# Another order of words in the front and in all passes, with one first-layer tile begun on three of four pairs of heads

## The chip, the cores and the metric

The kernel runs on one core of one Trainium2 chip. The metric is device microseconds for one execution, the median of several runs. TensorE (PE) multiplies matrices and writes into PSUM, eight banks of 512 fp32 columns. VectorE (DVE) and ScalarE (ACT) read PSUM and write SBUF; GpSimd (POOL) works on SBUF alone and issues most of the loads; SyncE (SP) issues stores and transposing DMAs. Every engine runs its own instructions in the order of the program and waits for the others by semaphores.

## The reference

Four batches of eight heads, 768 rows of 64 numbers. Rows are cut into chunks of 32; a chunk attends to its own 32 keys, 16 to the left, 8 to the right and 8 memory keys of its head. The result, laid out as 3072 tokens of 512 numbers, goes through two layers:

```python
for c in range(nc):                       # chunks of 32 rows
    k_full = concat(mem_k, k[l_start:r_end]); v_full = concat(mem_v, v[l_start:r_end])
    scores = q_c @ k_full.T / sqrt(64)
    a = softmax(scores); out[c] = a @ v_full
x = out.transpose(0, 2, 1, 3).reshape(3072, 512)
h = x @ w_in                              # 512 -> 2048
g = h + sin(alpha * h) ** 2 / (alpha + 1e-9)
y = g @ w_out                             # 2048 -> 512
```

## The kernel before, in words

**Passes.** There is a front, which prepares the attention of batch 0, and four passes, one for each batch. Pass i runs the two layers of batch i, and beside them the attention of batch i+1. The first layer is 16 tiles of 128 hidden features by 768 tokens. A tile takes a pair of PSUM banks (half 0 and half 1, 384 tokens each), and each half is four matmuls over the four k-tiles of `xT`; a k-tile is a pair of heads (`half_tile`, L422). Then ACT takes the sine (`sine`, L435), one of ACT, DVE or POOL squares it (`squared`, L441), and DVE adds it to the hidden value and writes `gT` (`finish`, L449), which gives the pair of banks back. The second layer (`second`, L458) multiplies `gT` by `w_out`, 96 matmuls of 512 columns for a batch, six token tiles of sixteen, each in one bank, copied out by ACT or DVE in turn (`close`, L467) and stored by SP.

**Words.** The order of the work is written out by hand. A stage runs a string of words; each word's first letter names a method of `Stage` (L503), the rest is its argument, and each method only issues instructions on the engines that it needs. The ones that matter here:

- `a`: cast one loaded pair of heads of batch 0 to bf16 (0 to 3 keys, 4 to 7 queries; the last letter is the engine, V for DVE, A for ACT). `k`, `l`: transpose a pair of heads of keys or queries on PE. `K`, `L`: copy that out of PSUM (`put_k`, `put_q`; after every `K`, DVE copies the two ends of the row, L291).
- `C`: constants. `Cb`, `Cm` the mask bias, `Ck` the memory keys, `Cl` alpha and its inverse, `Ci`, `Cp`, `Cz`, `Cv`, `Cs` fills on POOL. `We`, `Ws`: load ACT's table for the exponential or the sine by a dummy activation (L699). `z`: matmuls on zeros, 512 columns each (L686), which compute nothing.
- `s`, `v`: scores with exponential, and values with the division (`normed`, L350). In the front the two digits are the pair of heads and the half of the tokens. `t`, `T`: transpose one block of the result into `xT` by PE and copy it by DVE or ACT; `c`: the same by a transposing DMA.
- `b`, `h`: half 0 and half 1 of a first-layer tile (`h` also issues the sine). `q`: the square, its last letter the engine. `g`: `finish`. `p`, `P`: the first three k-tiles of a half ahead of the rest (`early`, L533); the strings of before do not use them.
- `f`: that many second-layer matmuls. `o`: hand the second layer of this pass to the feed, in groups of tokens; an `f` that asks for a matmul whose `gT` is not issued yet takes none. After the last pass the rest of the feed runs.
- `V`, `U`, `I`, `d`, `R`, `Z`, `X`, `m`, `H`: loads of values, of `w_out`, of `w_in`, of queries and keys, and the memory values; `V`, `U`, `I`, `d`, `R` are DMAs issued by POOL, and so stand in one queue with POOL's squares.

**PSUM.** `Banks` (L59) hands out, at the time the program is written, the pair that was given back longest ago. With four pairs in all, the fifth open tile must wait on the chip for a `finish` of an earlier one.

Of the kernel before, what the change touches and what calls it, by code (L numbers as in the profile page):

```python
# [11 lines left out]
NEG = -30000.0  # L12
CROSSED = {0: (0, 0), 1: (0, 0), 2: (1, 1), 3: (1, 1)}
KW = 1024
BF = mybir.dt.bfloat16
F32 = mybir.dt.float32
ACTF = mybir.ActivationFunctionType
ALU = mybir.AluOpType


class Feed:
# [64 lines left out]
def kernel(  # L86
# [20 lines left out]
    KT = d_model // P  # L107
# [14 lines left out]

    ident = consts.tile([P, P], BF, name="ident")
    biasm = consts.tile([P, 6], F32, name="biasm")
    mcol = consts.tile([P, P], BF, name="mcol")
    mrow = consts.tile([P, P], BF, name="mrow")
    asum = consts.tile([P, 8], BF, name="asum")
    mind = consts.tile([P, NJ, 3, 32], BF, name="mind")
    tiny = consts.tile([1, 1], F32, name="tiny")
    zeros = consts.tile([P, 512], BF, name="zeros")  # L130
    kTs = [consts.tile([P, HP, KW], BF, name=f"kT{i}") for i in range(2)]
    qTs = [consts.tile([P, HP, S], BF, name=f"qT{i}") for i in range(2)]
# [217 lines left out]
    def normed(otv, bs):  # L350
# [5 lines left out]
            in1=rinv[:].unsqueeze(3).to_broadcast([QW, 2, HP, D]),  # L356
            op=ALU.mult,
        )
# [61 lines left out]


    def half_tile(t, hf, k0=0, k1=4):  # L422
        for kt in range(k0, k1):
            nc.tensor.matmul(  # L424
                t["hT"][:, hf, 0:HALF],
                w_in_sb[:, kt, P * t["ft"]:P * t["ft"] + P],
                t["xT"][:, kt, HALF * hf:HALF * hf + HALF],
                start=(kt == 0), stop=(kt == KT - 1),
            )

    def opened(ft, xT):
        hT, bs = banks.pair()
        return {"ft": ft, "xT": xT, "hT": hT, "bs": bs, "from": [0, 0]}
# [7 lines left out]
    def squared(t, eng):  # L441
# [3 lines left out]
        else:  # L445
            e = nc.vector if eng == "V" else nc.gpsimd
            e.tensor_tensor(out=s2[:], in0=u[:], in1=u[:], op=ALU.mult)  # L447

    def finish(t, gT):  # L449
# [3 lines left out]
            in0=t["s2"][:], scalar=inv_alpha[:, ft:ft + 1], in1=t["hT"][:, :, 0:HALF],  # L453
            op0=ALU.mult, op1=ALU.add,
        )
# [47 lines left out]
    class Stage:  # L503
# [29 lines left out]
        def early(self, a, hf):  # L533
            if int(a) not in self.tile:
                self.tile[int(a)] = opened(int(a), self.next_x() if self.i < 0 else self.xT)
            t = self.tile[int(a)]
            half_tile(t, hf, 0, 3)
            t["from"][hf] = 3
# [6 lines left out]

        def do_b(self, a):
            if int(a) not in self.tile:
                self.tile[int(a)] = opened(int(a), self.xT)
            t = self.tile[int(a)]
            half_tile(t, 0, t["from"][0])  # L550

        def do_h(self, a):
            t = self.tile[int(a)]
            half_tile(t, 1, t["from"][1])
            sine(t)
# [175 lines left out]
    def const_b():  # L731
        for col, lo, hi in rows:
            nc.vector.tensor_reduce(
                out=biasm[:, col:col + 1], in_=ident[:, lo:hi], op=ALU.add, axis=mybir.AxisListType.X
            )
        for col in (0, 3):
            nc.vector.tensor_tensor(
                out=biasm[:, col:col + 1], in0=biasm[:, col:col + 1], in1=biasm[:, 5:6], op=ALU.add
            )
        nc.vector.tensor_scalar(  # L740
            out=biasm[:, 0:5], in0=biasm[:, 0:5], scalar1=-NEG, scalar2=NEG,
            op0=ALU.mult, op1=ALU.add
        )
# [59 lines left out]
    def const_s():  # L803
# [6 lines left out]
    first = {}  # L810
    stage = Stage(-1, None)
    stage.tile = first
    stage.run((
# [3 lines left out]
    ))  # L817
    for i, words in enumerate(((
# [6 lines left out]
    ),(  # L825
# [5 lines left out]
    ),(  # L831
# [5 lines left out]
    ),(  # L837
# [3 lines left out]
    ))):  # L841
        stage = Stage(i, stage.nx).run(words)
    feed.take(400)

# [28 lines left out]
```

## Time and profile before

| | |
|---|---|
| median of three runs | 215.29 us (214.83 to 215.68) |
| span of the profiled execution | 213.1 us; the runs lie 1.8 to 2.6 us above it, the median 2.2 |
| PE busy | 201.7 us, 95% |
| ACT, DVE, POOL busy | 143.5, 140.5, 99.8 us |
| first-layer matmuls (L424) | 512 |
| second-layer matmuls (L462) | 400 |
| first matmul of a first-layer tile | 24.81 us |
| last second-layer stretch of pass 3 begins | 189.32 us |

The span runs from the first to the last instruction; no time of the profiled execution itself beyond its span is given. Matmuls overlap, so a matmul's own duration is about twice the time until the next one starts, and PE's busy share says little; what counts is when each group starts and how many matmuls it holds. The idle time shown in brackets behind a row is that of its engine just before the row, with what ended it.

### The profile page before, as it was taken

To read this page: it belongs to the slowest core of one execution; us is meant where nothing else is said; L and a number is where in the kernel's file an instruction comes from. 1 tells how busy PE (TensorE), PEld (TensorE's weight loads), DVE (VectorE), ACT (ScalarE), POOL (GpSimd) and SP (SyncE) were. 2 spreads that over 40 slices of the span, in tenths; PEclk is the share of its full clock that TensorE was granted. 3 is DMA by queue.
4 is the path that set the end of the run, shared out by engine and by line. 5 is a ranking of instruction groups with operands and counts; after the bars stand their busy time and mean duration, and the time that the engine had idled before them with its cause. 6 is when DMAs were issued, how large, how long until landed. Compare 5 with 4: busy or idle time off the path is not lost.

```text
span 213.1 us, 4479 instructions
## 1 busy us (share of the span) xinstructions
PE 201.7 (95%) x1721; PEld 113.5 (53%) x1721; DVE 140.5 (66%) x218; ACT 143.5 (67%) x230; POOL 99.8 (47%) x140
## 2 busy tenths in 40 slices
PE   0799899999999999999999999999999999999994
PEld 0456555565455556555455555554555555554443
DVE  7598678999542749975856649898157197865011
ACT  2597898976857469977846199887846289891110
POOL 8959515688598193009991039659400023200000
PEclk9999999999999999999999999999999999999999
DMA  6999999999999999969999229989945400000312
GB/s 195 337 163 141 193 209 205 204 163 182 131 177 141 137 148 144 180 88 110 126 217 171 72 63 131 156 126 129 175 115 123 124 15 0 2 3 0 148 49 98
DMA packets 95908, 28.19 MB, mean 132 GB/s; under 512 B 84864, under 2 KB 92432, under 8 KB 95888
## 3 DMA queue, kind: packets, MB, share of 16 engines
q0 software_dynamic: 68736, 13.25, 92.3%
q1 hardware_dynamic: 26976, 14.62, 28.2%
q8 instruction: 13, 0.21, 0.4%
q14 instruction: 7, 0.06, 0.1%
q10 hardware_dynamic: 176, 0.04, 0.1%
HBM read 29.66 MB, written 6.29 MB: 169 GB/s over the span
## 4 chain that ended last, share of the span: by engine, by line
PE 71%; DVE 9%; DMA 7%; ACT 4%; issue 4%; POOL 3%; DVEq 0%; POOLq 0%; ACTq 0%
PE ps L462 38%; PE ps L424 27%; DMA memv_st<-in_mem_v_dram 4%; DVE gT L451 4%; DVE s L447 3%; DMA vw<-in_v_dram 3%; PE ps L414 3%; PE ps L385 2%; ACT u L439 2%; PE ps L366 1%; ACT s L444 1%; POOL s L447 1%; POOL vw L172 1%; DVE kT L285 1%; ACT L699 1%
## 5 line engine op out<-in xcount | busy, mean ns | idle before, releaser
L462 PE MATMUL ps<-w_out_sb,gT 128*128 128x512 bf16 (+2 forms) x400 | 89.1, 371 | 0.0
L424 PE MATMUL ps<-xT,w_in_sb 128*128 128x384 bf16 x512 | 86.0, 326 | 0.7 <-DVE gT L451 0.4
L451 DVE SCALAR_TENSOR_TENSOR gT<-s,inv_alpha,ps 128x768 bf16<-128x768 f32 x64 | 63.0, 1011 | 12.5 <-ACT s L444 5.2
L424 PEld LDWEIGHTS <-w_in_sb 128*128 128x128 bf16 x512 | 49.8, 98 | 35.4 <-issue 2.1
L439 ACT ACTIVATE u<-ps,alpha_sb 128x768 f32<-128x768 f32 x64 | 56.6, 895 | 16.8 <-PE ps L424 14.3
L462 PEld LDWEIGHTS <-gT 128*128 128x128 bf16 x400 | 36.6, 98 | 37.9 <-DVE gT L451 0.2
L447 POOL TENSOR_TENSOR s<-u 128x768 f32<-128x768 f32 x11 | 17.4, 1582 | 69.7 <-ACT u L439 69.7
L399 ACT ACTIVATE pt<-ps,biasm 128x256 bf16<-128x256 f32 x72 | 27.2, 489 | 10.5 <-PE ps L385 10.5
L469 DVE COPY o_sb<-ps 128x512 f32<-128x512 f32 (+1 forms) x15 | 10.1, 678 | 28.3 <-PE ps L462 26.4
L447 DVE TENSOR_TENSOR s<-u 128x768 f32<-128x768 f32 x23 | 21.9, 953 | 7.8 <-ACT u L439 7.8
L444 ACT ACTIVATE s<-u 128x768 f32<-128x768 f32 x30 | 25.0, 841 | 0.5
L354 DVE TENSOR_TENSOR x_blk<-ps,rinv 96x512 bf16<-96x512 f32 x32 | 22.0, 687 | 1.1
L469 ACT COPY o_sb<-ps 128x512 f32<-128x512 f32 (+1 forms) x10 | 5.6, 562 | 21.6 <-PE ps L462 21.6
L172 POOL DMA_DIRECT2D vw<-in_v_dram x13 | 12.9, 994 | 7.9 <-PE ps L366 5.4
L353 DVE RECIPROCAL rinv<-ps 96x8 f32<-96x8 f32 x32 | 6.4, 200 | 13.5 <-PE ps L414 12.7
L179 POOL DMA_DIRECT2D vw<-in_v_dram x13 | 12.7, 976 | 0.0
L238 POOL DMA_DIRECT2D kst<-in_k_dram x16 | 12.2, 760 | 1.1 <-DMA vw<-in_v_dram 0.8
L232 POOL DMA_DIRECT2D kst<-in_k_dram x16 | 11.3, 708 | 2.3 <-DMA vw<-in_v_dram 1.6
L369 ACT COPY xT<-ps 128x384 bf16<-128x384 bf16 x12 | 5.6, 496 | 8.2 <-PE ps L366 8.2
L245 POOL DMA_DIRECT2D q_bf<-in_q_dram x12 | 10.7, 912 | 0.0
L414 PEld LDWEIGHTS <-pt 128*128 128x128 bf16 x192 | 8.2, 97 | 4.2 <-ACT pt L399 0.3
L414 PE MATMUL ps<-vw,pt 128*128 128x65 bf16 x192 | 8.9, 193 | 0.0
(81 smaller groups left out, 131.4 us busy)
## 6 DMA issues: line engine op xcount, KB each, us to landing
out_dram<-o_sb SPq DMA_DIRECT2D x23, 256.0 KB, 2.3
kq_f<-in_k_dram SPq DMA_DIRECT2D x4, 384.0 KB, 6.5
kq_f<-in_q_dram SPq DMA_DIRECT2D x4, 384.0 KB, 6.0
q_bf<-in_q_dram POOLq DMA_DIRECT2D x12, 128.0 KB, 6.7
w_in_sb<-in_moe_w_in_dram POOLq DMA_DIRECT2D x1, 1152.0 KB, 12.6
vw<-in_v_dram POOLq DMA_DIRECT2D x7, 128.0 KB, 6.7
vw<-in_v_dram POOLq DMA_DIRECT2D x8, 112.0 KB, 7.4
kst<-in_k_dram POOLq DMA_DIRECT2D x14, 64.0 KB, 5.1
```

The source lines that it names most:

```text
L172: nc.gpsimd.dma_start(vw[0:64, lo:c1, 0:D], win(vflat, a, n, 64))
L179: nc.gpsimd.dma_start(vw[72:128, c0:hi, 0:D], win(vflat, base + QW * c0 + 48, hi - c0, 56))
L354: nc.vector.tensor_tensor(out=x_blk[:].rearrange("p g e d -> p e g d"), in0=otv[0:QW, :, :, 0:D], in1=rinv[:].unsqueeze(3).to_broadcast([Q ...
L399: nc.scalar.activation(pt[:, 0:H * QW].rearrange("p (g e c) -> p g e c", g=2, e=4)[:, :, :, 32 * m:32 * m + 32], sc[:, :, 0:4 * QW].rearra ...
L414: nc.tensor.matmul(otv[:, e, hp, :], pt[:, QW * i:QW * i + P], vws[b % 2][:, 2 * hp + e, j, 0:D + 1],)
L424: nc.tensor.matmul(t["hT"][:, hf, 0:HALF], w_in_sb[:, kt, P * t["ft"]:P * t["ft"] + P], t["xT"][:, kt, HALF * hf:HALF * hf + HALF], start= ...
L439: nc.scalar.activation(t["u"][:], t["hT"][:, :, 0:HALF], ACTF.Sin, scale=alpha_sb[:, ft:ft + 1])
L444: nc.scalar.activation(s2[:], u[:], ACTF.Square)
L447: e.tensor_tensor(out=s2[:], in0=u[:], in1=u[:], op=ALU.mult)
L451: nc.vector.scalar_tensor_tensor(out=gT[:, ft, :].rearrange("p (e c) -> p e c", e=2), in0=t["s2"][:], scalar=inv_alpha[:, ft:ft + 1], in1= ...
L462: nc.tensor.matmul(o[:, c0:c1], gT[:, ft, P * s:P * s + P], w_out_sb[:, ft, c0:c1], start=(ft == 0), stop=(ft == FT - 1),)
L469: copier(state["engines"][state["o"] % len(state["engines"])])(o_sb[:, c0:c1], o[:, c0:c1])
```

## The change

The front's string is replaced (`FRONT`), and so are the four passes' (`PASSES`).

- In the front, POOL's fill `Ci` comes first; DVE casts `a0`, `a4` right after the mask bias and takes alpha's constants (`Cl`) later; `K1`, `L0` and `K3` go from ACT to DVE, `L1`, `K2` and `a7` from DVE to ACT; the first four `z` stand ahead of `Cm`, a fifth joins the second four, and one ends the front; at the end `T20` and `T31` become DVE copies (`t`), `t21` becomes an ACT copy, and the sine's table load `Ws` stands before them.
- `half_tile` takes the k-tiles in the order 0, 1, 3, 2 (`KTS`), in all tiles. `p1` in the front issues the first three matmuls of half 0 of tile 1, which need pairs of heads 0, 1 and 3, before the pair 2 is transposed. In pass 0 `b1` then issues one matmul in place of four. `do_b` may now open a tile in the front.
- In the passes, second-layer words are cut into smaller ones and moved by a few places, some `b`, `h` and `g` change places with a neighbour, and some squares and copies change engine: pass 0 `q8` ACT to POOL, `q15` and `K2` DVE to ACT, with the copies `T3` and `T7` to DVE and `t5` to ACT; pass 1 `q14` ACT to DVE; pass 2 `q12` DVE to ACT, `q14` ACT to POOL; pass 3 `q6` ACT to DVE, `q10` and `q15` ACT to POOL, `q13` DVE to ACT, `q14` ACT to DVE. On POOL's queue `q8` thereby comes ahead of a load of `w_out` and one of values.

The numbers of matmuls, of `z` and of bytes moved stay the same.

```diff
@@ -12,10 +12,42 @@
 NEG = -30000.0
 CROSSED = {0: (0, 0), 1: (0, 0), 2: (1, 1), 3: (1, 1)}
 KW = 1024
+KTS = (0, 1, 3, 2)
 BF = mybir.dt.bfloat16
 F32 = mybir.dt.float32
 ACTF = mybir.ActivationFunctionType
 ALU = mybir.AluOpType
+FRONT = (
+    'Ci Cb a1A z4 Cp Cm a0V a4V eVA Cz k0 Cv K0V a5A dm Ck a2A Cl We l0 k1 l1 V024 L0V K1V s00 a6V L1A '
+    'V002 a3V k2 K2A s11 s01 a7A V068 l2 s10 k3 z1 m0 z4 L2A Cs K3V v10 V046 z1 l3 I02 L3A v11 s20 v01 '
+    's30 s31 v00 s21 v30 T10 v31 T01 v20 T00 T30 v21 Ws p1 t20 I27 t11 T21 eVA t31 z1 '
+)
+PASSES = ((
+    'b0 o8 h0 I7g b1 U69 q0V h1 U12 dq108 q1A b4 h4 b3 g0 g1 h3 dk108 q4V b6 g4 b2 q3A h2 g3 Ufg U01 h6 '
+    'b5 h5 b7 h7 q5A q2V q6P U56 q7P g2 g6 b10 h10 U24 q10A g5 b9 h9 g7 b8 h8 q8P U45 V158 g10 b13 b11 '
+    'h13 q9V h11 g9 g8 l0 l2 L0A L2A q13P l3 q11V Ube g11 k2 K2A U9b Uef b15 h15 b12 q15A f1 h12 f1 f1 '
+    'g13 f1 g15 q12A f1 b14 g12 h14 f2 V125 k0 k1 l1 k3 L3A K1V f2 K0A L1V f3 K3A f1 q14V f1 g14 f2 m1 f1 '
+    'V102 s61 f2 f1 f1 f3 f8 s70 s3 f1 f2 f1 f1 f2 f1 f1 f1 f1 f1 v0 v6 c6 f4 v3 f1 f1 f7 s542 f1 t3 f1 '
+    'f1 f1 f1 f1 f1 f3 f1 f1 v7 f3 v4 v1 f2 v2 T0 f2 c4 c2 f2 f1 f1 f2 f1 f2 T1 v5 f1 f2 f2 f1 T5 Ws f4 '
+    'f1 f2 t7 f2 f2 '
+), (
+    'o1 b0 h0 f1 q0V R2 b3 g0 Ws h3 q3A b1 g3 h1 R4 q1V b2 h2 q2A g1 b5 h5 b4 h4 g2 Ws q4A q5V b6 h6 q6A '
+    'R8 g5 g4 b8 Ws h8 g6 R1 q8V b9 dy h9 q9A Z b7 R3 V378 h7 g8 V226 b11 g9 h11 b10 h10 q10A f1 q7V f1 '
+    'R4 Ws f1 f5 X8 q11A g7 f1 g10 b12 f1 h12 g11 b14 q12P b13 h13 g12 h14 f2 f1 f1 V202 f1 q13A q14V f1 '
+    'g13 f1 b15 X6 g14 h15 eV f1 f2 f3 f3 We s24 f2 f3 f4 q15V g15 f1 V268 f6 s05 s1 f3 f2 m2 f2 v4 f2 f5 '
+    'f1 f1 v1 f4 v0 v2 f1 f4 c4 f4 f1 f1 s63 s7 f1 t1 c2 f5 v6 V357 T0 f1 f2 v3 f4 v7 f1 f1 c7 f2 v5 t3 '
+    'f2 f13 t5 f2 f2 T6 '
+), (
+    'b0 b3 Ws R9 R1 h0 h3 q0V b5 h5 Ws b1 R1 q5A g0 R2 q3P h1 Ws g3 g5 f2 q1A b2 h2 b4 g1 R1 q2V R1 h4 b6 '
+    'b7 g2 R1 f1 q4A f1 h6 h7 Z b9 g4 h9 R1 b8 R2 q6V R1 eV o1 q7P h8 q8A X1 g6 b11 h11 g7 q9P g9 b10 '
+    'q11A h10 b13 h13 g8 g11 b12 b14 q10V X3 g10 h14 V305 h12 q13P q14P g13 R1 f9 q12A b15 g12 f1 eAV R1 '
+    'H3 f1 f1 h15 g14 f2 q15V g15 X8 f1 s24 f17 s103 f8 v4 f1 f1 v0 f1 f1 X1 f1 f1 X1 f1 c4 v3 f1 c3 f1 '
+    'v2 f1 c2 f5 c0 s675 f9 f1 v1 c1 f4 Ws v7 f2 v5 f1 c7 v6 f1 f1 c6 f1 c5 f3 f1 f11 f2 f1 f1 f1 f3 '
+), (
+    'b2 b0 h2 q2V h0 q0A b4 b3 h4 g2 g0 h3 q4V b1 h1 o2 q1A g4 Ws b6 h6 q3P g3 g1 b8 h8 q6V b5 h5 g6 q5A '
+    'b7 h7 q8P b11 g8 h11 g5 q7V g7 q11P b10 h10 b9 h9 q9A b12 h12 q10P g11 g10 q12A b15 h15 q15P g9 b13 '
+    'h13 b14 g12 h14 q13A g13 q14V g15 g14 '
+))
 
 
 class Feed:
@@ -420,12 +452,13 @@
 
 
     def half_tile(t, hf, k0=0, k1=4):
-        for kt in range(k0, k1):
+        for n in range(k0, k1):
+            kt = KTS[n]
             nc.tensor.matmul(
                 t["hT"][:, hf, 0:HALF],
                 w_in_sb[:, kt, P * t["ft"]:P * t["ft"] + P],
                 t["xT"][:, kt, HALF * hf:HALF * hf + HALF],
-                start=(kt == 0), stop=(kt == KT - 1),
+                start=(n == 0), stop=(n == KT - 1),
             )
 
     def opened(ft, xT):
@@ -545,7 +578,7 @@
 
         def do_b(self, a):
             if int(a) not in self.tile:
-                self.tile[int(a)] = opened(int(a), self.xT)
+                self.tile[int(a)] = opened(int(a), self.next_x() if self.i < 0 else self.xT)
             t = self.tile[int(a)]
             half_tile(t, 0, t["from"][0])
 
@@ -810,35 +843,8 @@
     first = {}
     stage = Stage(-1, None)
     stage.tile = first
-    stage.run((
-        'a1A Cb Cp Cz Cv a5A eVA Cm Cl z4 a0V Ci k0 dm a4V l0 k1 K0V Ck l1 L0A V024 We L1V a2A K1A V002 '
-        'a6V k2 s00 K2V a3V s11 V068 m0 a7V s01 l2 s10 k3 K3A L2A V046 z4 v10 l3 Cs L3A I02 v11 s20 z1 '
-        'v01 s30 z1 v00 s31 z1 v30 s21 v31 T01 T10 v20 T30 T00 v21 T20 T31 I27 t11 t21 eVA Ws '
-    ))
-    for i, words in enumerate(((
-        'o8 b0 h0 I7g q0V U69 U12 b1 h1 dq108 q1A b4 h4 b3 g0 h3 b6 g1 dk108 q4V g4 q3A b2 h2 h6 b5 h5 '
-        'Ufg g3 b7 q2V U01 U56 q6P h7 g2 q5A b10 U24 q7P g6 h10 b9 q10A g5 h9 U45 b8 h8 g7 g10 q8A q9V '
-        'V158 b11 h11 g9 b13 g8 h13 l0 l2 l3 L0A L2A q13P k2 q11V Ube b15 U9b g11 Uef g13 K2V h15 b12 '
-        'q15V h12 q12A b14 g15 f7 h14 V125 k1 k0 g12 l1 K1V k3 L1V L3A q14V K3A K0A V102 f9 g14 s61 f16 '
-        'm1 s70 s3 f13 v0 f3 v6 c6 f6 v3 f5 s542 T3 f10 T0 v4 f6 v2 f2 v1 c4 c2 f7 v7 f1 T1 f3 v5 Ws T7 '
-        'f8 t5 '
-    ),(
-        'b0 o1 h0 b3 R2 q0V h3 b1 Ws q3A g0 g3 h1 q1V b2 R4 h2 q2A b5 h5 b4 h4 Ws g1 g2 q5V g5 b6 q4A h6 '
-        'R8 Ws g4 b8 q6A g6 h8 R1 b9 q8V dy h9 b7 q9A g8 Z h7 R3 V378 b11 h11 b10 g9 V226 h10 R4 q7V Ws '
-        'q10A f2 X8 q11A g7 f8 b12 h12 g10 g11 b14 h14 q12P g12 b13 h13 V202 q13A g13 q14A f7 X6 b15 g14 '
-        'h15 f7 eV We s24 q15V f6 g15 f7 V268 s05 s1 f1 m2 f14 v4 v1 f6 v0 f1 v2 f2 c4 f6 s63 s7 t1 f4 c2 '
-        'v6 V357 T0 f4 v3 f4 v7 c7 v5 t3 f17 t5 T6 '
-    ),(
-        'b3 Ws R9 b0 h0 R1 h3 b5 h5 Ws R1 b1 q5A q0V g0 R2 q3P g3 h1 Ws q1A b2 h2 g5 R1 g1 b4 h4 R1 b6 '
-        'q4A q2V h6 g2 R1 Z b7 h7 b9 h9 R1 g4 R2 q6V b8 g6 R1 eV o1 h8 q7P g7 q8A b11 h11 X1 q11A q9P b10 '
-        'g9 g8 h10 b13 g11 h13 q10V g10 b14 h14 b12 q13P X3 V305 h12 g13 q12V q14A R1 f8 eAV b15 g12 '
-        'R1 H3 h15 f6 g14 q15V X8 s24 f16 g15 f2 s103 f9 v4 v0 f3 X1 f2 X1 c4 v3 f2 c3 v2 f1 c2 f6 c0 '
-        's675 f10 v1 f4 c1 Ws f1 v7 v5 c7 v6 f2 c6 c5 f24 '
-    ),(
-        'b2 h2 q2V b0 h0 b4 q0A g2 h4 b3 h3 g0 o2 b1 h1 Ws q3P b6 q4V q1A h6 g4 b8 h8 g3 b5 g1 q6A h5 q5A '
-        'b7 g6 h7 b11 q8P g8 h11 b10 g5 q7V h10 q10A q11P b9 h9 q9A g7 g11 b12 h12 b15 g10 q12A h15 g9 '
-        'g12 b13 h13 b14 q15A h14 g15 q14A q13V g14 g13 '
-    ))):
+    stage.run(FRONT)
+    for i, words in enumerate(PASSES):
         stage = Stage(i, stage.nx).run(words)
     feed.take(400)
 
```

## The prediction

> **What bounds the kernel now.** I read the page's busy shares first, then the chain of waits in order of time, then PE's rows in order of time, and last the front on all engines.
>
> ```profile
> PE 201.7 (95%) x1721; PEld 113.5 (53%) x1721; DVE 140.5 (66%) x218; ACT 143.5 (67%) x230; POOL 99.8 (47%) x140
> PE 71%; DVE 9%; DMA 7%; ACT 4%; issue 4%; POOL 3%; DVEq 0%; POOLq 0%; ACTq 0%
> ```
>
> PE is the bound: it holds 71% of the chain that ended last. The rest of the chain is in the front and in a few places after it. The chain itself (start, duration, what):
>
> ```profile
> 14.34 1.75 POOL vw L172
> 16.09 6.06 DMA vw<-in_v_dram
> ...
> 22.29 0.43 PE ps L344 x8
> ...
> 25.05 1.28 ACT L699
> 26.35 0.20 ACT tiny L699
> 26.55 0.79 ACT u L439
> ...
> 34.68 1.02 DVE gT L451
> 35.70 0.04 issue
> 35.74 6.70 PE ps L424 x40
> ...
> 75.64 10.45 PE ps L424 x64
> ...
> 162.69 5.61 PE ps L462 x26
> ```
>
> The front waits for the last values (DMA until 22.15), then for ACT's table load at 25.05; the first sine starts behind it, and DVE, square and finish in turn, is late from there until 35.70, when it hands PE the pair of banks that it waits for. So whatever the first sine loses or gains up to there, PE loses or gains at 35.74. The two last rows give PE's pace where nothing waits: 10.45/64 = 163 ns for a first-layer matmul, 5.61/26 = 216 ns for a second-layer one.
>
> PE's rows, each group with its start and count, show what PE loses after the front:
>
> ```profile
> 24.81 17.62 PE L424 MATMUL ps<-xT,w_in_sb 128*128 128x384 bf16 x104
> 42.36 1.29 PE L274 MATMUL ps<-ident,q_bf 128*64 128x128 bf16 x36
> ...
> 51.14 2.17 PE L462 MATMUL ps<-w_out_sb,gT 128*128 128x512 bf16 x9
> 53.52 0.51 PE L385 MATMUL ps<-qT,kT 64*128 64x96 bf16 x16 [0.20 <-DVE kT L291]
> ...
> 122.06 13.39 PE L424 MATMUL ps<-xT,w_in_sb 128*128 128x384 bf16 x80
> 135.61 6.75 PE L424 MATMUL ps<-xT,w_in_sb 128*128 128x384 bf16 x40 [0.15 <-DVE gT L451]
> ...
> 168.14 11.86 PE L424 MATMUL ps<-xT,w_in_sb 128*128 128x384 bf16 x72
> 180.22 9.26 PE L424 MATMUL ps<-xT,w_in_sb 128*128 128x384 bf16 x56 [0.22 <-DVE gT L451]
> ```
>
> From the start of one group to the next, less count times pace: 17.55 - 104 x 0.163 = 0.6 us in pass 0; 2.38 - 9 x 0.216 = 0.44 before the first scores; 13.55 - 80 x 0.163 = 0.5 in pass 2; 12.08 - 72 x 0.163 = 0.35 in pass 3. That is 1.9 us, and it bounds what all the moves after the front can win. What they can lose has no such bound.
>
> **The front, step by step.** The rows that carry it:
>
> ```profile
> 4.90 0.23 DVE L754 COPY mrow<-ps 128x128 bf16<-128x128 bf16 x1 [0.38 <-PE ps L753]
> 6.28 1.89 PE L686 MATMUL ps<-zeros 128*128 128x512 bf16 x4
> 6.77 0.50 DVE L653 CAST k_bf<-kq_f 128x768 bf16<-128x768 f32 x1
> 8.10 0.85 PE L274 MATMUL ps<-ident,k_bf 128*64 128x128 bf16 x12
> 10.43 0.82 ACT L653 CAST k_bf<-kq_f 128x768 bf16<-128x768 f32 x1
> 11.04 0.36 DVE L207 COPY kT<-memkT 128x256 bf16<-128x256 bf16 x2
> 11.76 0.34 PE L317 MATMUL ps<-mind,mrow 64*128 64x384 bf16 x2
> 12.31 3.04 ACT L332 ACTIVATE pt<-ps 128x768 bf16<-128x768 f32 x4 [0.45 <-PE ps L325]
> 14.93 1.04 PE L686 MATMUL ps<-zeros 128*128 128x512 bf16 x4
> 15.24 0.71 ACT L285 COPY kT<-ps 128x672 bf16<-128x672 bf16 x1
> 15.84 0.82 ACT L299 COPY qT<-ps 128x768 bf16<-128x768 bf16 x1
> 21.89 0.86 ACT L369 COPY xT<-ps 128x384 bf16<-128x384 bf16 x2
> 23.89 0.69 DVE L354 TENSOR_TENSOR x_blk<-ps,rinv 96x512 bf16<-96x512 f32 x1
> 24.63 0.34 PE L366 MATMUL ps<-ident,x_blk 96*128 96x96 bf16 x4 [0.15 <-DVE x_blk L354]
> ```
>
> *Earlier keys.* `a0` now follows the mask copy and starts at 5.15 instead of 6.77. Its transposes waited behind four zeros until 8.10, 0.83 after the cast's end; those zeros now run long before. So the key chain, which ended with the memory keys at 11.40, ends 1.62 + 0.83 = 2.45 earlier, at 8.95. Then come alpha's constants, three short DVE instructions and a trip to PE and back, which I estimate at 1.0 from the mask's own trip (its copy sat idle 0.38 for PE). `L0`, now on DVE and behind them, ends about 11.15. The first scores then start at 11.2 (11.76 before), the first exponential 0.55 later: 11.75 instead of 12.31.
>
> *More ACT work after that.* The first four exponentials ran back to back, to 15.35. Between them now stand `L1` (0.82), `K2` (0.71) and `a7` (0.82), less about 0.1 each that neighbours overlap: 2.05. The fourth ends at 11.75 + 3.04 + 2.05 = 16.85, 1.5 later than before. From there to the table load ACT has two query copies (1.64), four exponentials (3.04) and four block copies (1.72), 6.4 in all, and about 0.5 of waiting for the transposes behind the first values: the load starts at 23.75 instead of 25.05. It was at 25.05 because of waits on PE and two more copies, so the longer list still fits, with 1.3 to spare.
>
> *The end of the front.* The values of pair 2 are bound by the DMA at 22.15, which the change leaves alone: the same eight POOL loads stand ahead, and `m0` on DVE still waits for the same load. The last normalised block ends at 24.58 as before, its transposes start at 24.63. But before, tile 0 followed after one group of four transposes (24.81). Now there are two groups and a zero matmul (0.17 + 0.17 + 0.26): tile 0 starts at 25.2. Its eight matmuls take 1.3, and ACT follows the last one's start by 0.35: first sine at 26.7 instead of 26.45 to 26.55. The early table load gains nothing by itself: in its place PE is late. So the first sine is **+0.2**; with DVE behind by what its three block copies and a slower exponential chain add, I take **+0.3**. Bounds: -0.4 if the values land half a microsecond earlier, +1.0 by the second rival below. `p1` saves 3 x 163 ns = 0.49 of PE, but in the gap that DVE sets at 35.74, so it buys nothing there; without it tile 1's sine would be 0.5 later.
>
> **The passes.** *k-tiles 0, 1, 3, 2*: same matmuls at the same pace, 0; the late piece of `xT` is read last, which covers `t20`.
>
> *Pass 0.* Through the second square group the order of DVE is unchanged, so the 0.6 stays, moved by +0.3. Before the first scores, DVE copied the last key ends at 53.04 to 53.45 behind a square; now those copies stand ahead of tile 14's square and finish, `K2` is on ACT, and ten second-layer matmuls stand between. The 0.44 goes: **-0.4**. What is late next there is ACT's exponentials, which have 12 matmuls (2.6 us) of cover. `q8` on POOL holds up the loads queued behind it:
>
> ```profile
> 38.06 0.59 POOL L219 DMA_DIRECT2D w_out_sb<-in_moe_w_out_dram  x1
> DMA to landing us min/median/max: 8.7/8.7/8.7
> ```
>
> This load of `w_out` tile 4 goes from 38.06 to about 42.8, landing 46.8 before; it is read near 48. If it took the same 8.7 it would land at 51.5 and PE would stand 3.5. But it sat behind earlier transfers; a later issue meets a shorter queue, so I take 0, with 0 to 3.5 as ends. `q13` on POOL then ends near 47 (45.3 before), covered by DVE's other finishes.
>
> *Passes 1 and 2.* The order of tiles, squares and finishes up to the stalls is the same, and so are the table loads ahead: 0 in both. The regions with attention hold PE at pace before and after; the finer `f` words there have values, copies and stores that are ready, cover 1 us or more: 0.
>
> *Pass 3.* DVE sat idle 1.13 for ACT's square of tile 6:
>
> ```profile
> 178.29 0.83 ACT L444 ACTIVATE s<-u 128x768 f32<-128x768 f32 x1
> 179.16 2.86 DVE L451 SCALAR_TENSOR_TENSOR gT<-s,inv_alpha,ps 128x768 bf16<-128x768 f32 x3 [1.13 <-ACT s L444]
> ```
>
> `q6` on DVE fills that with 0.95, but `b0` ahead of `h2` delays the first sine and all of DVE's list behind it by four matmuls, 0.65. DVE's finish of tile 6 ends at 178.03 + 0.65 + 0.95 + 1.0 = 180.6 at worst, 180.4 with the idle 0.29 it had for POOL; it was 180.18. **+0.2**, between -0.35 (the stall goes) and +0.6.
>
> **Sum.** +0.3 - 0.4 + 0 + 0 + 0.2 = +0.1 on a span of 213.1, and 2.2 of surroundings as the median has: **215.4 us**, no change. A measurement of this kernel tells no change from one beyond 0.5% (1.1 us).
>
> **A rule against the front.** Four zeros took 1.89 us at 6.28 and 1.04 at 14.93: PE ran at half speed first. With the zeros at 1.2 PE then stands nearly idle until 9.3, so its twelve-transpose groups cost 0.85, not 0.53, up to the first scores. The Trainium skill, TensorE: Matmul & The Clock Gate, Part 1, says that full rate comes after about 3.4 us of sustained work and is lost after an idle window of that length; the rows agree (6.09 to about 9.5). By it the first exponential would come at about 12.1; by warm rows 11.75. The 1.3 to spare on ACT takes either, so the sum stands.
>
> **Rivals.**
> 1. *Faster: the values land early and the stalls in pass 2 or 3 go.* The early keys shift DVE's casts away from POOL's issue at 14.34, which took 1.75 where others take 0.9; at 0.9 the values land at 21.3, the first sine at 26.0 (-0.5), pass 0 -0.4, and pass 3's stall -0.35: 215.3 - 1.25 = **214.0**. Against it: `m0` still runs on DVE just then.
> 2. *Slower: ACT sets the front.* If PE stays cold and the first exponential comes at 13.0, the spare 1.3 is gone; each microsecond beyond is one of the first sine. With half-speed score and value groups between the later exponentials (0.3 each, four times) the first sine is at 27.9, +1.4: **216.6**. It decides once the fourth exponential ends past 18.2.
> 3. *Slower: the late `w_out` load* holds PE at the fifth second-layer matmul of pass 0, 1 to 3.5 us, **217**. The queue's backlog until 45.85 speaks against it.
> 4. *Nothing of it reaches PE* beyond 0.2 us: **215.3**.
>
> **How the numbers follow.** My sum with rival 4: 0.46. Rival 1, or parts of it: 0.30. Rival 2: 0.14; rival 3: 0.10. Forecast and rival 4 lie within 0.5%, rival 1 is faster, 2 and 3 slower. The range leaves out the far ends of 1 and 3: 213.8 to 216.7; the likeliest alone 214.6 to 216.1.
>
> **What would show it.** The first sine at 26.7; the table load at 23.7; tile 0's matmuls at 25.2; the group of forty matmuls at 36.0; scores of pass 0 without a wait on the key ends; PE's gap in pass 3 near 180.6, and pass 2's unchanged. I am wrong if the fourth exponential ends after 18, if PE waits on `w_out` near 48, or if a pass has a gap over 0.6 us that before has not.

## The result, and the profile after

The changed kernel takes **228.12 us** (median of 4, 226.6 to 229.18) where the kernel before takes 215.45 (median of 4): a ratio of 1.058, 95% interval 1.053 to 1.064. It is 12.7 us slower; the forecast was 215.4, no change. Ratios, here and below, leave out executions that lie over 1.5% behind the fastest of the same kernel; medians keep them. The profiled execution is the quickest of the four (226.6 us); its span is 224.5 us, 11.4 more than that of before, and these 11.4 are what the account below divides.

The page of the changed kernel (busy times, TensorE's granted clock in 40 slices, the chain that ended last by engine):

```profile
PE 207.9 (93%) x1721; PEld 116.1 (52%) x1721; DVE 141.4 (63%) x219; ACT 140.9 (63%) x225; POOL 105.1 (47%) x144
PEclk9999999999999999999589999999999999999999
PE 52%; DMA 14%; SPq 11%; DVE 10%; issue 5%; POOL 4%; ACT 3%; DVEq 0%; ACTq 0%; POOLq 0%
```

PE's share of the chain fell from 71% to 52%, while DMA rose from 7% to 14% and SP's queue, absent before, came in at 11%. PE's busy time grew by 6.2 us with the same 1721 matmuls: some of them ran slower, and one slice of the clock line shows 5 tenths.

Where the time went is read from the start of the same first-layer matmul in both kernels, at the start of each pass. Of before, the row that the prediction did not show:

```profile
75.48 3.78 PE L424 MATMUL ps<-xT,w_in_sb 128*128 128x384 bf16 x22
```

Of after, PE's rows at the starts of passes 1, 2 and 3:

```profile
77.98 1.30 PE L457 MATMUL ps<-xT,w_in_sb 128*128 128x384 bf16 x7
130.75 4.55 PE L457 MATMUL ps<-xT,w_in_sb 128*128 128x384 bf16 x27
178.95 3.25 PE L457 MATMUL ps<-xT,w_in_sb 128*128 128x384 bf16 x19
```

Against 75.48, 122.06 and 168.14 PE is late by 2.50, 8.69 and 10.81 us, and 11.4 at the end. With 2.06 us from the front (the group that started at 35.74 starts at 37.80 in the chain of waits), the account is: **front +2.1, pass 0 +0.4, pass 1 +6.2, pass 2 +2.1, pass 3 +0.6**. The largest term is in a pass that the forecast put at nothing.

**Pass 1.** While PE computes pass 1, the keys and queries of the next batch are loaded as rows and turned by fourteen DMA transposes on SP's queue, and the scores at the pass's end read them. SP's rows before:

```profile
72.50 3.96 SPq L472 DMA_DIRECT2D out_dram<-o_sb  x2
76.54 0.91 SPq L253 DMA_DIRECT2D kst<-memv_st  x1
80.76 10.73 SPq L260 DMA_TRANSPOSE kT<-kst  x8
91.58 8.49 SPq L263 DMA_TRANSPOSE qT<-q_bf  x6
```

The same rows of SP after:

```profile
75.87 3.87 SPq L505 DMA_DIRECT2D out_dram<-o_sb  x2
79.83 0.91 SPq L285 DMA_DIRECT2D kst<-memv_st  x1
87.20 10.88 SPq L292 DMA_TRANSPOSE kT<-kst  x8
98.16 7.98 SPq L295 DMA_TRANSPOSE qT<-q_bf  x6
```

PE's rows of after at the scores:

```profile
105.84 0.34 PE L417 MATMUL ps<-qT,kT 64*128 64x96 bf16 x8 [1.06 <-DMA qT<-q_bf]
108.61 0.50 PE L417 MATMUL ps<-qT,kT 64*128 64x96 bf16 x8 [2.42 <-DMA qT<-q_bf]
109.04 4.88 PE L495 MATMUL ps<-w_out_sb,gT 128*128 128x512 bf16 x11
```

And a window of after just behind them (its columns: busy time and instructions of PE, of its weight loads, of DVE, ACT and POOL, then the granted clock, the DMA share and GB/s):

```profile
109.00:113.80 4.80, 4.80 (x15) 1.50 (x11) 2.37 (x3) 1.20 (x3) 3.36 (x4) 0.50 2.55 144
```

The small copy of the memory rows into `kst` is issued 3.3 us later than before, of which PE's own lateness is 2.5; but the first transpose, which needs it, starts 6.4 us later. Before, PE came to these scores at 101.83 and found them ready:

```profile
101.83 0.51 PE L385 MATMUL ps<-qT,kT 64*128 64x96 bf16 x16
```

After, PE stands 1.06 + 2.42 = 3.5 us for the last turned queries. And when it goes on, the clock is granted at 0.50 (the trace's clock records have it so from 107.11, while PE still waits, to 113.94): 4.88/11 = 444 ns for a second-layer matmul that takes 216, another 11 x 0.228 = 2.5 us. Together that is the 6 us of this pass.

What stands ahead on SP and POOL explains the later issue. Before, ACT's table load was over when the last output tile of pass 0 came; after, it stands in the way. Two rows of ACT before:

```profile
73.22 1.28 ACT L699 ACT_TABLE_LOAD   x1
...
75.51 0.59 ACT L469 COPY o_sb<-ps 128x512 f32<-128x512 f32 x1 [0.44 <-PE ps L462]
```

POOL's first value load before:

```profile
73.87 0.69 POOL L172 DMA_DIRECT2D vw<-in_v_dram  x1 [5.39 <-PE ps L366]
```

The same of ACT after:

```profile
77.42 1.28 ACT L732 ACT_TABLE_LOAD   x1
...
78.83 0.56 ACT L502 COPY o_sb<-ps 128x512 f32<-128x512 f32 x1
```

And of POOL after:

```profile
75.72 0.69 POOL L204 DMA_DIRECT2D vw<-in_v_dram  x1 [4.45 <-PE ps L446]
```

The output copy, and so the store on SP and everything behind it, comes 3.3 us later; POOL's value loads, which wait for PE's last values of the pass (before, the profile names the block transposes right behind them), only 1.85. So the memory rows' copy went out 76.54 - 73.87 = 2.67 us behind the first value load before and 79.83 - 75.72 = 4.11 after, among loads that are then already under way. The DMA share (the time that packets took, over the engines' time, so that it can pass 1) is 1.44 from the copy's issue to the first transpose before; after, it is 1.76 to 83.5 us and 3.25 from there to the first transpose.

**Pass 2.** The two value loads `V305` stand ahead of POOL's square of tile 13 instead of behind it. POOL's rows before:

```profile
140.77 1.52 POOL L447 TENSOR_TENSOR s<-u 128x768 f32<-128x768 f32 x1 [3.58 <-ACT u L439]
142.23 1.28 POOL L172 DMA_DIRECT2D vw<-in_v_dram  x1
```

After, the first of the loads and the square on POOL:

```profile
145.83 1.28 POOL L204 DMA_DIRECT2D vw<-in_v_dram  x1
...
149.46 1.50 POOL L480 TENSOR_TENSOR s<-u 128x768 f32<-128x768 f32 x1 [1.08 <-ACT u L472]
```

And what PE then waits for:

```profile
156.66 0.34 PE L417 MATMUL ps<-qT,kT 64*128 64x96 bf16 x8 [1.08 <-DMA qT<-q_bf]
157.51 0.35 PE L417 MATMUL ps<-qT,kT 64*128 64x96 bf16 x8 [0.50 <-DMA qT<-q_bf]
```

PE is 8.7 us late there, so loads that kept their place would start at 150.9; they start at 145.83. The first four transposes of the queries are then in flight with them and land a median 7.5 us after issue, where before it was 3.3. The two waits make 1.6 of this pass's 2.1 us; what is left is not traced to its cause.

**The front.** PE stayed at half pace until about 18.4 us. PE's rows of after:

```profile
5.56 0.85 PE L306 MATMUL ps<-ident,k_bf 128*64 128x128 bf16 x12 [1.72 <-DVE k_bf L686]
7.98 0.27 PE L804 MATMUL ps<-ident,memv_st 16*128 16x16 bf16 x4 [1.57 <-DVE memv_st L800]
9.29 0.28 PE L818 MATMUL ps<-ident_f,alpha_rows 16*128 16x16 f32 x1 [1.03 <-DVE ident_f L815]
...
16.59 0.85 PE L306 MATMUL ps<-ident,k_bf 128*64 128x128 bf16 x12
17.37 1.73 PE L719 MATMUL ps<-zeros 128*128 128x512 bf16 x5
...
19.50 0.53 PE L306 MATMUL ps<-ident,q_bf 128*64 128x128 bf16 x12
```

ACT's rows of after:

```profile
16.70 0.81 ACT L364 ACTIVATE pt<-ps 128x768 bf16<-128x768 f32 x1
...
20.06 0.80 ACT L331 COPY qT<-ps 128x768 bf16<-128x768 bf16 x1 [1.86 <-PE ps L306]
...
28.91 1.71 ACT L472 ACTIVATE u<-ps,alpha_sb 128x768 f32<-128x768 f32 x2 [1.10 <-PE ps L457]
```

A group of twelve transposes still takes 0.85 us at 16.59 and 0.53 at 19.50; before, it was at 0.53 from 10.71 on. ACT ends its fourth exponential at 17.51, copies one pair of queries, then sits idle 1.86 us for the next query transposes, which PE reaches late, behind five slow zero matmuls. First sine: 28.91.

**Pass 3.** DVE waits 0.24 us for a square of POOL three times, at 187.31, 191.48 and 195.64. The first of them in DVE's rows of after:

```profile
187.31 1.94 DVE L484 SCALAR_TENSOR_TENSOR gT<-s,inv_alpha,ps 128x768 bf16<-128x768 f32 x2 [0.24 <-POOL s L480]
```

### The profile page after: what moved, and what is told of

Its sections match the earlier page's. It is cut to its first block, busy times and chain, and to the rows that moved or that the text cites. A ratio compares the mean times of both kernels' runs of the same rounds, so it can differ in the third digit from the quotient of the medians.

```text
span 224.5 us, 4487 instructions
## 1 busy us (share of the span) xinstructions
PE 207.9 (93%) x1721; PEld 116.1 (52%) x1721; DVE 141.4 (63%) x219; ACT 140.9 (63%) x225; POOL 105.1 (47%) x144
## 4 chain that ended last, share of the span: by engine, by line
PE 52%; DMA 14%; SPq 11%; DVE 10%; issue 5%; POOL 4%; ACT 3%; DVEq 0%; ACTq 0%; POOLq 0%
PE ps L495 31%; PE ps L457 10%; DMA qT<-q_bf 8%; SPq L292 6%; SPq L295 4%; DVE gT L484 4%; DMA q_bf<-in_q_dram 3%; DVE s L480 3%; PE ps L306 3%; PE ps L446 2%; ACT u L472 2%; PE ps L417 2%; DMA kq_f<-in_k_dram 2%; DMA kst<-in_k_dram 1%; POOL q_bf L277 1%
## 5 line engine op out<-in xcount | busy, mean ns | idle before, releaser
L495 PE MATMUL ps<-w_out_sb,gT 128*128 128x512 bf16 (+2 forms) x400 | 92.7, 378 | 0.0
L457 PE MATMUL ps<-xT,w_in_sb 128*128 128x384 bf16 x512 | 87.2, 326 | 1.5 <-DVE gT L484 0.6
L480 POOL TENSOR_TENSOR s<-u 128x768 f32<-128x768 f32 x15 | 23.6, 1577 | 81.0 <-ACT u L472 81.0
L480 DVE TENSOR_TENSOR s<-u 128x768 f32<-128x768 f32 x23 | 22.8, 993 | 9.7 <-ACT u L472 9.6
L477 ACT ACTIVATE s<-u 128x768 f32<-128x768 f32 x26 | 21.9, 842 | 0.6
L204 POOL DMA_DIRECT2D vw<-in_v_dram x13 | 12.0, 922 | 6.1 <-PE ps L446 4.4
L211 POOL DMA_DIRECT2D vw<-in_v_dram x13 | 12.4, 957 | 1.1 <-DMA vw<-in_v_dram 1.1
L417 PE MATMUL ps<-qT,kT 64*128 64x96 bf16 x192 | 6.2, 207 | 5.3 <-DMA qT<-q_bf 5.3
L401 ACT COPY xT<-ps 128x384 bf16<-128x384 bf16 x10 | 4.8, 484 | 9.7 <-PE ps L398 9.4
```

The lines of the kernel that those rows point to most:

```text
L457: nc.tensor.matmul(t["hT"][:, hf, 0:HALF], w_in_sb[:, kt, P * t["ft"]:P * t["ft"] + P], t["xT"][:, kt, HALF * hf:HALF * hf + HALF], start= ...
L477: nc.scalar.activation(s2[:], u[:], ACTF.Square)
L495: nc.tensor.matmul(o[:, c0:c1], gT[:, ft, P * s:P * s + P], w_out_sb[:, ft, c0:c1], start=(ft == 0), stop=(ft == FT - 1),)
```

## The experiments

Each is the changed kernel or the kernel before with words moved; the arithmetic is the same in all, but the three runs with the warm front have two zero matmuls more. Ratios are to the kernel before on the same chip in the same session. "Late by" compares PE's start of the same first-layer matmul with the profiled kernel before.

### Front and passes apart

```diff
 e1_front: the changed kernel
-PASSES = (new words of passes 0 to 3)
+PASSES = (old words of passes 0 to 3)
```

> The changed front and k-tile order with the old words in all four passes. Theory (three separate losses: TensorE at half clock in the front, 2.1 us; late q transposes in pass 1, about 5.6 us; the same in pass 2, 2.1 us): only the front's 2.1 us stay, 215.45 + 2.1 = 217.5 us. Rival (the stalls in passes 1 and 2 are only the front's lateness handed on to transfers that are issued late): they come back, 223 us or more.

Measured 216.18 us, ratio 1.004 (0.999 to 1.008). The front was late by 0.92 in this profile, not 2.1, because PE came to full pace at about 14 us: its zeros at 15.99 took 1.25 us for five. Pass 1 had one wait of 0.98 us on the turned queries. So a late front alone makes no stall of 3.5 us, and the new words of the passes hold most of the loss.

```diff
 e2_passes: the changed kernel
-FRONT = (new words)
+FRONT = (old words)
```

> The old front with the new words in all four passes. Theory (separate losses): 228.1 - 2.1 = 226.0 us, with PE's waits on the transposed q in passes 1 and 2 as they were. Rival (the front's lateness makes the stalls): 215.5 to 217.5 us.

228.98 us, ratio 1.057 (1.048 to 1.066): the theory's number was missed, and its rival's far more. PE left the front only 0.45 late, but waited 1.65 + 2.51 us in pass 1 and 3.00 in pass 2. In pass 1 PE reached the scores 1.6 us earlier than in the changed kernel, but the last turned queries came only 0.9 earlier, so it waited longer: it leaves the pass late by 8.05 us, against 8.69. In pass 2 the one long wait was followed by half clock, which the changed kernel's 1.08 + 0.50 was not, and the pass lost 5.6 us. The front is not on the path that sets the end of the changed kernel.

### The front

```diff
 e3_warm: FRONT of the changed kernel
-Ci Cb a1A z4 Cp Cm a0V a4V eVA Cz k0 Cv K0V a5A dm Ck a2A
+Ci Cb a1A Cp Cm a0V a4V eVA Cz k0 z4 Cv K0V a5A dm Ck z2 a2A
```

> The changed kernel with the first four zero matmuls moved behind the first key transposes and two more behind the memory keys, so that TensorE does not sit idle from 6.4 to 9.3. Theory (TensorE's clock sets the front): transposes take 0.53 instead of 0.85 from about 10 us on, the fourth exponential ends by 16.5 instead of 17.5, the first sine comes at 27.0 instead of 28.9, time 226.3 us. Rival (ScalarE's list of copies and casts between the exponentials sets the front whatever the clock): first sine 28.5 or later, 227.5 to 228.5 us.

PE's rows of this run:

```profile
6.34 1.89 PE L719 MATMUL ps<-zeros 128*128 128x512 bf16 x4
...
11.78 0.53 PE L306 MATMUL ps<-ident,k_bf 128*64 128x128 bf16 x12
...
157.51 0.34 PE L417 MATMUL ps<-qT,kT 64*128 64x96 bf16 x8 [2.64 <-DMA qT<-q_bf]
```

Its first sine among ACT's rows:

```profile
26.90 1.72 ACT L472 ACTIVATE u<-ps,alpha_sb 128x768 f32<-128x768 f32 x2 [1.09 <-PE ps L457]
```

The front did what the clock theory said: full pace from 11 us, first sine at 26.90 instead of 28.91, and PE late by 0.05 us instead of 2.06 after it. The time did not follow: 228.27 us, ratio 1.056 (1.049 to 1.063), since PE lost 7.5 us in pass 1 and 4.9 in pass 2. In pass 2 its first wait is now 2.64 us long (0.17 more follow eight matmuls later), and the clock was granted at 0.50 behind it; with 1.08 + 0.50 it was not.

One profile tells a front's price only roughly. Eight profiles with the new front and its early zeros left it late by 0.67 to 2.51 us; three with the warm front by 0.05, 0.46 and 0.87; five others with the old front by -0.25 to 0.93.

### Pass 1

```diff
 e5_p0old: the changed kernel
-PASSES[0] = new words
+PASSES[0] = old words
 e6_p1old: the changed kernel
-PASSES[1] = new words
+PASSES[1] = old words
```

> The changed kernel with the old words in pass 0. Theory A (pass 0's new tail puts the last output stores, and behind them on SP's queue the copy of the memory rows into kst, about 0.8 us later against POOL's value loads; that copy then lands 6 instead of 4 us after its issue and all fourteen transposes behind it start late): the wait in pass 1 falls from 3.5 us and 2.1 us of half clock to about 1 us, 223 us. Rival B (pass 1's own words make it): 227.5 to 228.5 us, wait as before.

> The changed kernel with the old words in pass 1. Theory A (pass 0's tail): the wait in pass 1 stays at 3 us or more, 227 to 229 us. Rival B (pass 1's words): it falls to 1 us or less, 222 to 223.5 us.

With pass 0's old words 220.25 us, ratio 1.019 (1.013 to 1.025); with pass 1's 228.45, ratio 1.056 (1.046 to 1.064). In the first the memory rows' copy stands 2.68 us behind the first value load, as before the change, and PE does not wait in pass 1; in the second it stands 4.12 behind, and PE waits 3.81 + 2.13 us. The words that make PE wait in pass 1 are those of pass 0. The time fell further than theory A had it (223), because no wait at all was left in pass 1. Pass 2 still waits: 2.30 + 0.20 us and half clock behind them in the profiled execution, the longest of the four (222.33 us).

```diff
 e7_v226: PASSES[1] of the changed kernel
-b7 R3 V378 h7 g8 V226 b11 g9
+b7 R3 V378 h7 g8 b11 g9
...
-f1 V202 f1
+f1 V226 V202 f1
```

> The changed kernel with the 480 KB of value loads V226 moved in pass 1 from ahead of the four q loads to just ahead of V202, some 20 us later on POOL's queue. Theory (these loads crowd the small copy of the memory rows out of the DMA engines): the copy lands 3 to 4 us after its issue instead of 6 to 7, the transposes start at 84 instead of 87.2, the wait in pass 1 falls from 3.5 us to under 1 us and no half clock follows, 223 us. Rival (the copy is late for what stands ahead of it on SP's queue): 227.5 us or more.

229.72 us, ratio 1.066 (1.062 to 1.069): the theory's number was missed. The first transpose began 6.1 us after the copy's issue instead of 7.4, at 86.41, yet the last turned queries were still 3.28 us late. Taking 480 KB out of the way is not enough when the copy is still issued 4.11 us behind the first value load and the loads return while the queries are being turned (here eight value loads go out from 100.33 to 107.6, in the changed kernel six from 99.87 to 105.0).

```diff
 e9_ws: PASSES[0] of the changed kernel
-T1 v5 f1 f2 f2 f1 T5 Ws f4
+T1 v5 Ws f1 f2 f2 f1 T5 f4
```

> The changed kernel with pass 0's sine table load (word Ws) put back ahead of the last copy of xT on ScalarE. Theory (the load, standing between PE's last second-layer matmul and the copy of the last output tile, holds SP's queue for 0.8 us, and with it the memory rows' copy and all fourteen transposes): the copy of the memory rows is issued 3.3 instead of 4.1 us behind the first value load and lands 1 to 3 us earlier against PE; the wait in pass 1 falls below 2 us, 223 to 226 us. Rival (the value loads, released earlier by the values' order, make the delay alone): wait of 3 us or more, 227.5 to 229 us.

SP's rows of this run:

```profile
78.38 0.91 SPq L285 DMA_DIRECT2D kst<-memv_st  x1
84.99 11.07 SPq L292 DMA_TRANSPOSE kT<-kst  x8
```

And PE's wait in pass 1:

```profile
105.79 0.35 PE L417 MATMUL ps<-qT,kT 64*128 64x96 bf16 x8 [1.39 <-DMA qT<-q_bf]
```

223.79 us, ratio 1.037 (1.031 to 1.042), in the theory's range. By the medians one word, the place of a table load, is worth 4.3 us of the 12.7: the copy goes out 3.3 us behind the first value load (75.06), PE waits 1.39, and no half clock follows.

```diff
 e10_wslate: PASSES[0] of the kernel before
-v5 Ws T7 f8 t5
+v5 T7 Ws f8 t5
```

> The kernel before with one word of pass 0 moved: the sine table load behind the copy T7 instead of ahead of it. Theory: the last output copy on ScalarE comes about 0.8 us later, the memory rows' copy with it, the transposes by 1 to 3 us; before, PE reached them with less than 1 us to spare, so pass 1 gets a wait of 0.5 to 3 us: 216 to 220 us. Rival (the order in pass 0 as a whole is needed): 215.0 to 215.9 us, no wait.

215.7 us, ratio 1.0005 (0.998 to 1.003): no effect, the rival's number. It does not speak against the mechanism, since it did not set it off: the copy went out 2.82 us behind the first value load (77.49 and 74.67), against 2.67 before. My edit did not delay the output store by the 0.8 us that I had expected.

```diff
 e13_z2: the changed kernel
 PASSES[0]
-h14 f2 V125
+h14 f2 dy V125
...
-v1 f2 v2 T0 f2 c4 c2
+v1 f2 v2 Z2 T0 f2 c4 c2
 PASSES[1]
-b9 dy h9 q9A Z b7
+b9 h9 q9A b7
```

`Z2` issues the memory rows' copy of batch 2 from within pass 0; `dy` loads the memory keys that it reads.

> The changed kernel with one transfer of pass 1 given earlier: the copy of the memory rows into kst (and the load of the memory keys it reads) stands on SP's queue ahead of the two xT transposes and the last two output stores of pass 0 instead of behind them. Theory (its place behind the late last store, and its landing among the value loads, start the fourteen transposes late): the first transpose starts within 1 us of the last store's issue, at 80 to 81 instead of 87.2, the wait in pass 1 is under 1 us with no half clock behind it, 222 to 223.5 us. Rival (the q loads on POOL's queue and the crowded transposes make the wait, whenever the first transpose starts): wait of 2 us or more, 226 to 228.5 us.

SP's rows of this run:

```profile
71.25 0.91 SPq L285 DMA_DIRECT2D kst<-memv_st  x1
...
75.69 3.74 SPq L505 DMA_DIRECT2D out_dram<-o_sb  x2
79.61 14.70 SPq L292 DMA_TRANSPOSE kT<-kst  x8
```

And PE at the scores:

```profile
104.40 0.51 PE L417 MATMUL ps<-qT,kT 64*128 64x96 bf16 x16
```

220.66 us, ratio 1.025 (1.017 to 1.034), below the theory's range. One small transfer is issued earlier on its queue; the transposes start at 79.61, the scores wait for nothing, and the whole 6.2 us of pass 1 is gone (PE is late by 2.18 before the pass and by 2.14 after it). So the cause was that copy, issued late behind a late store. The other runs say the same in steps: where the copy is issued 2.7 to 2.8 us behind the first value load (seven profiles), the first transpose follows it by 4.1 to 4.8 us; at 3.32 (e9) by 6.6; at 4.1 (six profiles) by 6.1 to 8.0. What in the DMA engines holds the copy that long, no run takes apart.

### Pass 2

```diff
 e4_v305: PASSES[2] of the changed kernel
-X3 g10 h14 V305 h12 q13P q14P
+X3 g10 h14 h12 q13P V305 q14P
 e11_v305early: PASSES[2] of the kernel before
-q13P X3 V305 h12
+X3 V305 q13P h12
```

> The changed kernel with one word of pass 2 moved: the two value loads V305 behind POOL's square of tile 13 again, as before the change. Theory (these loads, issued some 5 us earlier against PE, crowd the q transposes out of the DMA engines): the last q transposes land about 3 us after issue instead of 6.4, PE's wait of 1.1 + 0.5 us at 155.4 goes, 226.2 us. Rival (the transposes are late because their issue on SP's queue is late): the wait stays, 228.1 us.

> The kernel before with one word of pass 2 moved: the value loads V305 ahead of POOL's square of tile 13. Theory (they crowd the last q transposes): a wait of 1 to 3 us on the transposed q in pass 2, 216.7 to 218.5 us. Rival (it takes the changed kernel's other orders): 215.0 to 215.9 us.

Moved back in the changed kernel: 225.69 us, ratio 1.043 (1.035 to 1.051), and pass 2 loses 0.6 us instead of 2.1; its first four query transposes land a median 3.8 us after issue again. Moved forward in the kernel before, the one word costs 7 us: 222.65, ratio 1.034 (1.031 to 1.037), far over what I expected.

POOL's rows of the second run:

```profile
137.02 1.28 POOL L201 DMA_DIRECT2D vw<-in_v_dram  x1
...
140.66 1.50 POOL L477 TENSOR_TENSOR s<-u 128x768 f32<-128x768 f32 x1 [1.09 <-ACT u L469]
```

And PE's:

```profile
149.23 0.34 PE L414 MATMUL ps<-qT,kT 64*128 64x96 bf16 x8 [2.68 <-DMA qT<-q_bf]
151.63 0.50 PE L414 MATMUL ps<-qT,kT 64*128 64x96 bf16 x8 [2.06 <-DMA qT<-q_bf]
152.06 6.68 PE L492 MATMUL ps<-w_out_sb,gT 128*128 128x512 bf16 x17
```

The loads are issued at 137.02 instead of 142.23, the first four query transposes land a median 8.9 us after issue instead of 3.3, PE stands 4.7 us, and its next 17 matmuls take 393 ns each. Before, POOL's square, waiting for ACT, held these loads back until the first four query transposes were nearly through. That wait looked idle and was useful.

### Pass 3, and all repairs together

```diff
 e12_p3: the kernel before
-PASSES[3] = old words
+PASSES[3] = new words
```

> The kernel before with the new words of pass 3 alone. Theory (squares on POOL, 1.5 to 1.9 us each, in place of 0.9 on the others hand tiles to VectorE late): three gaps of 0.3 us at PE, +0.6 us, 216.0 us. Rival (the gaps come from the lateness of what stands before pass 3): 215.0 to 215.6 us.

216.7 us, ratio 1.005 (1.001 to 1.008). PE loses the same 0.6 us within pass 3 (late by 2.40 at its start, 3.01 at its end), so it belongs to the pass's own words. In all eleven profiles with these words PE loses 0.60 or 0.61 us there; in the five others besides before, 0.17 at most.

```diff
 e8_combo: the changed kernel
 FRONT of e3_warm, PASSES[2] of e4_v305
-PASSES[0] = new words
+PASSES[0] = old words
 e14_best: the changed kernel
 FRONT of e3_warm, PASSES[0] and [1] of e13_z2, PASSES[2] of e4_v305
-PASSES[3] = new words
+PASSES[3] = old words
```

> The changed kernel with the warm front, the old words in pass 0 and V305 behind the square of tile 13. Theory A (losses in three places, each undone): 215.5 + 0.6 for pass 3 + 1 for what is left of pass 1's wait = 217 us. Rival B (pass 1's words make that wait, and a front that is earlier only makes TensorE wait longer for the transposes): 222 to 225 us.

> All repairs together: warm front, memory rows' copy early, V305 behind the square of tile 13, old words in pass 3; what is left of the change is the front's order, the k-tile order and the new words of passes 0, 1 and 2. Theory (four places explain the whole loss): 215.0 to 216.3 us, no difference from before. Rival (something else of the change still costs): 217 us or more.

216.82 us, ratio 1.005 (1.002 to 1.009), and 216.21, ratio 1.003 (1.001 to 1.006). With all four places mended (e14) the loss is gone but for some 0.3%, and nothing else of the change costs or gains more than that. Neither version beats the kernel before.

```diff
 e15_bz: the kernel before
 PASSES[0]
-f7 h14 V125
+f7 h14 dy V125
...
-T0 v4 f6 v2
+T0 v4 f6 Z2 v2
 PASSES[1]
-q8V dy h9
+q8V h9
...
-g8 Z h7
+g8 h7
```

> The kernel before with the copy of the memory rows given early in the same way. Theory (before, the transposes come just in time in passes 1 and 2, so that an earlier start gains nothing in most executions): 214.5 to 215.9 us. Rival (part of before's time is this wait): 213 to 214.3 us.

216.13 us, ratio 1.0015 (0.998 to 1.005), no difference: before the change the transposes came in time.

## Why the prediction was wrong, step by step

**Front, +0.3 forecast, +2.1 measured.** The step that failed is "the 1.3 to spare on ACT takes either, so the sum stands". I saw that PE would stand nearly idle until 9.3, but let it be slow only up to the first scores; it stayed slow to about 18.4 us, and everything that PE does for ACT up to there came late. The second rival had the mechanism (216.6 from this alone), though not the mark by which it would show: the fourth exponential ended at 17.51, inside the 18.2 that I had named, and the loss came after it, at the query transposes: I had allowed 0.5 us of waiting there, and ACT waited 1.86. The Trainium skill, TensorE: Matmul & The Clock Gate, Part 1, has full rate come after about 3.4 us of sustained work. In the trace PE is busy without a gap from 9.29 to 13.60 and again from 13.98, and full pace begins at 18.37: later than by the rule read plainly, and the last section shows why. Moving the four early zeros (at 1.2 us) behind the first transposes and adding two (e3) gave back the 2.0 us. That this profile shows 2.1 is partly chance: the same front cost 0.67 to 2.51.

**Pass 0, -0.4 forecast, +0.4 measured.** The wait before the first scores did go. In its place PE waited for a bank pair that DVE finished late. In DVE's rows of after:

```profile
45.60 1.53 DVE L480 TENSOR_TENSOR s<-u 128x768 f32<-128x768 f32 x1
```

And in PE's:

```profile
48.30 0.81 PE L457 MATMUL ps<-xT,w_in_sb 128*128 128x384 bf16 x4 [0.49 <-DVE gT L484]
```

A square of DVE took 1.53 us instead of 0.95 just ahead of it. "Through the second square group the order of DVE is unchanged" stopped one group too early. Why the square took longer is not shown. All nine profiles with the new words of pass 0 have this wait (0.48 or 0.49 us); the old pass 0 has none at this place behind the new front (e1, e5). The late load of `w_out` (the third rival) did not bite.

**Pass 1, 0 forecast, +6.2 measured.** This is the step that decided: "the order of tiles, squares and finishes up to the stalls is the same, and so are the table loads ahead: 0 in both". I followed the table load of each pass only to the next sine, and not to the output copy and the store behind it. On SP's queue that store stands ahead of the memory rows' copy and of fourteen transposes whose slack I never measured. None of my rivals names SP's queue or the transposes. The rows that would have told were there: transposes issued until 91.58 + 8.49 = 100.07, for scores that PE reaches at 101.83.

**Pass 2, 0 forecast, +2.1 measured.** I counted `V305` as ready loads with a microsecond of cover for their reader. What counted was not when they are read but what they ride over: the queries being turned.

**Pass 3, +0.2 forecast, +0.6 measured.** Upper bound 0.6, and shown on its own in e12. The stall that I had `q6` filling went, and three waits on POOL's squares came.

**k-tile order, 0.** It agrees with e1 and e14, in which it stands; no run changes it alone.

The likeliest fault in the method: I priced moves on POOL and SP by the engine time that they take, and by who reads their result, but not by the queue that stands behind them.

## What to carry to other kernels

When a kernel is bound by one engine and a queue of transfers runs just in time beside it, list for each queue what its last reader has to spare, before pricing any move on the compute engines. A table load, a copy or a square that moves by one place can hold or release a queue, and a wait of a few microseconds costs more than its length when the clock falls behind it. A wait on an idle engine may be what keeps a load from riding over a transfer that matters.

## What the runs showed that I had not expected

**The price of a wait on PE.** Behind waits of 1.06 + 2.42 us (eight score matmuls between them) the granted clock was 0.50 until 113.94; behind one of 2.64 (e3, pass 2) it was 0.50 too; behind 1.39 (e9) and 1.08 + 0.50 matmuls ran at full pace. So the wait of 3.5 us in pass 1 cost 6. The Trainium skill, TensorE: Matmul & The Clock Gate, Part 1, has half rate follow an idle window of about 3.4 us. Here a window that is mostly idle was enough. In all these traces a stretch of half clock behind the front lasts 3.41 us, or two or three times that. If each trace is cut into pieces of 3.41 us, counted from its first clock record, a full clock fell behind every piece in which PE was busy for at most 44% of the time (12 pieces ahead of the kernels' ends, 10% to 44%), and behind none in which it was busy for 47% or more. So what a wait costs hangs on where it falls as well as on its length: 2.30 us brought half clock (e5, pass 2, a piece 33% busy); 1.79 + 0.36 us, which fell into two pieces (66% and 71% busy), did not (e9, pass 2).

**How far the warm-up varies.** With the same instructions in the front, twelve transposes first took 0.53 us at 14.64 in one execution (e1) and at 19.50 in another (the changed kernel). The same cutting shows the difference: in e1 a piece that ended at 14.00 was 90% busy, and full pace followed; in the changed kernel a piece that ended at 14.95 was 89% busy, and full pace came only a piece later, at 18.37. It was that close: a piece of 89% did bring full pace in e9. The clock records begin where full pace does, at 18.37 in the changed kernel; the 1.00 that a window shows ahead of that is no record, so pace there has to be read from the durations.

**Transposes among loads.** Over the run, a transpose of queries landed a median 3.3 us after issue before the change and 7.1 after it, with the same transposes. For the first four of pass 2, e11 and e4 show the cause: one word that moves two value loads ahead of them or back takes their median from 3.3 to 8.9 us and from 7.5 to 3.8.
